# Score tiles as 64-row products on two row groups, and a batch's rows brought out of PSUM head by head on ScalarE

## The chip, the core and the metric

The kernel runs on one core of a Trainium2 chip. The metric is the device time of one launch, in microseconds, as a median of several runs. The core's engines are TensorE (in the profile PE for products and PEld for its weight loads), VectorE (DVE), ScalarE (ACT) and GpSimd (POOL); SP is the queue from which nearly all transfers are issued. Each engine works through its instructions in the order in which the program wrote them and waits at semaphores for the others.

## What is computed

The reference is attention with a top-32 mask, followed by a mixture of experts on its output:

```
scores = scale * q @ k.T                  # 8 batches, 8 heads, 576 tokens, 64 wide
kth    = 32nd largest of each row
attn   = softmax(where(scores >= kth, scores, -1e9))
x      = (attn @ v) as 4608 rows of 512
logits = x @ w_gate + modality_bias[modality_id]
e      = argmax(logits);  g = softmax(logits)[e]
out    = g * (relu(x @ w1[e]) @ w2[e])    # 8 experts, 1024 hidden
```

Everything is float32. The choice of the 32 largest and of the expert hangs on small differences, so the scores are computed to nearly full float32 precision.

## The kernel before

Two heads make a pair, and there are 32 pairs. The 1152 query rows of a pair are cut into nine tiles of 128 rows; tiles 0 to 7 belong to one head each (even tiles to head 0, odd ones to head 1), and tile 8 holds the last 64 rows of both heads. One step of the main loop (`for i in range(LAST)`, 288 tiles and some more) writes the work of several tiles at different stages: the scores of tile `i + 2`, the search for the 32nd largest of tile `i`, the probabilities, the transposes and the evacuation of earlier tiles, the product with v of an earlier pair, the preparation of the next pair, and a share of the expert work. Four pairs make a batch of 36 steps. The order on each engine is this program order; there is no scheduler behind it.

**Scores.** `prep` transposes q and k and splits each into a part `hi` of type float32r and the rest `lo` (`split`), into a tile `st` whose partitions 0 to 63 hold head 0 and 64 to 127 head 1. Six transfers on SP (`stack`, L313) then write `ks`, in which both halves of the 128 partitions hold the same 64 rows of k, and four more (L315) write `qs`, with `hi` of q in the lower half and `lo` in the upper. A product of 128 rows of `qs` with `ks` so adds two of the four terms hi·hi, lo·hi, hi·lo, lo·lo at once. `qk` (L371) makes a normal tile of four such products, two for each half of 288 key columns; tile 8 takes its q from `qbd`, in which the two heads stand apart (GpSimd, `fill`, L324), in four products of 512 columns and four of 64. The tile goes to one PSUM tile `S` of two banks (a single buffer), and ScalarE copies it to SBUF (`sevac`, L378). The first pair is scored without stacking, by 64-row products straight from its `st` (`unstacked`, L355), two tiles at a time: tile S from the lower row group, tile T from the upper.

**Other TensorE work of a step.** The transposes of the probabilities (L481), the transposes and the remainder of the split in `prep` (L290, L297, L276), the product with v in 64-column groups (`av`, L509), the gate's products in 32-column groups (L554), the turning back of a batch's rows (`xrow`, L542), and the experts (L775, L787).

**Rows of a batch.** When a batch's four pairs are done, five steps of `xrow` transpose its output back to token rows, and VectorE takes the PSUM tile X out, times 1 over the softmax sum `rd` (L543), as an entry of the list `late`.

**Pacing.** Expert work of slots of 256 rows stands in a list `moe`, and each step takes pieces from it as long as a balance is positive: the step adds `STEP` = 3.39 and takes off what the table `COST` says of its own TensorE work. A slot may begin when enough batches are done. Where the list is empty, or no batch is done yet, `keep_warm` issues a few products that nobody reads. Thirteen slots are done in this way; the rest come in a last part with products split in three terms (L1005, L1021).

Of the kernel before, what the change touches and what calls it, by code (L numbers as in the profile page):

```python
# [53 lines left out]
COST = {"trans": 0.5, "qk": 0.5, "mix": 1.02, "rest": 0.22, "t": 0.11, "prep": 0.43, "logits": 1.2, "xrow": 0.54, "av": 0.49, "av8": 0.17}  # L54
# [18 lines left out]
def kernel(  # L73
# [40 lines left out]

    LD, PR, T = {}, {}, {}
# [57 lines left out]
    qbd = [[o.tile([128, 128], FR, name=f"qbd{i}{j}", bufs=1) for j in range(2)] for i, o in enumerate((const, wk))]  # L173
    for a in qbd:
        for t in a:
            V.memset(t.bitcast(FT), 0.0)
# [88 lines left out]
    late, late_pe = [], []  # L265
# [14 lines left out]
    def prep(p, part, first=False):  # L280
# [3 lines left out]
        if first:  # L284
            d.setdefault("st", st0)
        elif "st" not in d:
            d["st"] = wk.tile([128, 2, 2, S], FR, name="st", bufs=1)
# [16 lines left out]
        if part == "k":  # L304
            d["ks"] = wk.tile([128, 2, 2, S], FR, name="ks", bufs=2)
        else:
            d["qs"] = wk.tile([128, 2, S], FR, name="qs", bufs=2)

        def stack(h, queues=(SP, SP)):
            for v in range(2):  # L310
                if part == "k":
                    for a, b, o in ((0, S, 0),) if h == 0 else ((0, 512, 64), (512, S, -512)):
                        queues[v].dma_start(d["ks"][half(v), :, h, a + o:b + o].bitcast(FT), st[half(h), :, a:b].bitcast(FT))  # L313
                else:
                    queues[v].dma_start(d["qs"][half(v), h, :].bitcast(FT), st[half(h), v, :].bitcast(FT))  # L315

        for h in range(2):
            f = lambda h=h, **o: stack(h, **o)
# [14 lines left out]
    st0 = wk.tile([128, 2, 2, S], FR, name="ks", bufs=2)  # L333
    bd0 = wk.tile([128, 2, S], FR, name="qs", bufs=2)[:, 0, :256].rearrange("p (x s) -> p x s", x=2)

    def fill_first():
        for h in range(2):
            r = slice(h * 64, h * 64 + 64)
# [717 lines left out]
    for i in range(LAST):  # L1056
# [25 lines left out]
        if ok(u):  # L1082
            sign(u)
# [320 lines left out]
```

## Time and profile before

| | |
|---|---|
| median of 3 runs | 1266.87 us (1263.65 to 1268.3) |
| the profiled execution | 1262.36 us, span 1260.6 us |
| TensorE busy (products) | 1181.1 us, 94% |
| VectorE busy | 1140.2 us, 90% |
| ScalarE busy | 989.0 us, 78% |
| GpSimd busy | 677.8 us, 54% |
| 16 DMA engines, mean share | 51.2% for SP's queue, 199.28 MB in all |

Busy time is the time in which an engine's instructions run as the profile has them. A product's record lasts until its result is out, and the next one starts well before that, so the rate of TensorE is read from the starts of its records and not from their lengths. A float32 product of 256 or 512 columns stands in the trace as two records. The span has a start of about 33 us, the main loop to about 1110 us, and the last part.

### The profile page before, as it was taken

What the parts mean: (1) busy time and instruction counts of PE and PEld (TensorE: products, weight loads), DVE (VectorE), ACT (ScalarE), POOL (GpSimd) and SP (SyncE); (2) the same over time, 40 slices, a digit from 0 to 9 for tenths busy, and PEclk for the clock granted to TensorE, in tenths of its full rate; (3) what the DMA queues carried; (4) which work ended last, traced back from release to release, by engine and by line L of the source; (5) the groups of instructions that cost most, each with busy time, mean ns of one, the idle gap of its engine ahead of it and who ended that gap; (6) DMA issues with size and microseconds to landing.
All of it is one profiled execution on the core that took longest, in us unless ns stands there. A gap on an engine that the chain in (4) does not pass through costs nothing. (4 is left out here: it accounts for less than half of the span.)

```text
span 1260.6 us, 28788 instructions
## 1 busy us (share of the span) xinstructions
PE 1181.1 (94%) x8032; PEld 927.0 (74%) x8032; DVE 1140.2 (90%) x5917; ACT 989.0 (78%) x2014; POOL 677.8 (54%) x1253
## 2 busy tenths in 40 slices
PE   7889987899988999989999999999999999999985
PEld 5667766768766868677777778787778775699885
DVE  6999999999999999999999999999999996477751
ACT  4999988889888988888898888888888885256542
POOL 4888865564574557554755466556755573211110
PEclk7999999999999999999999999999999999999998
DMA  4563337754356745655666566656576425478550
GB/s 107 156 186 86 87 86 224 199 150 126 86 136 188 217 117 157 189 156 139 171 184 177 146 182 191 185 154 169 161 207 178 128 71 168 150 251 275 190 174 15
DMA packets 204339, 199.28 MB, mean 158 GB/s; under 512 B 104413, under 2 KB 151533, under 8 KB 204160
## 3 DMA queue, kind: packets, MB, share of 16 engines
q1 hardware_dynamic: 196880, 177.96, 51.2%
q0 software_dynamic: 6080, 19.00, 4.2%
q8 instruction: 69, 1.13, 0.4%
q14 instruction: 110, 0.90, 0.2%
q10 hardware_dynamic: 1200, 0.30, 0.1%
HBM read 118.63 MB, written 24.23 MB: 113 GB/s over the span
## 5 line engine op out<-in xcount | busy, mean ns | idle before, releaser
L385 DVE MAX8 cand<-Ssb 128x8 f32<-128x82 f32 (+1 forms) x2016 | 429.5, 230 | 5.4 <-ACT Ssb L378 5.4
L423 POOL TENSOR_TENSOR y<-Ssb,K 128x576 f32<-128x576 f32 x288 | 370.4, 1286 | 5.7 <-ACT K L417 5.4
L417 ACT ACTIVATE K<-Ssb,n 128x576 bf16<-128x576 f32 x288 | 227.2, 789 | 29.0 <-POOL y L423 28.2
L378 ACT ACTIVATE Ssb<-S 128x576 f32<-128x576 f32 x284 | 185.9, 655 | 80.9 <-PE S L371 45.5
L371 PE MATMUL S<-ks,qs 128*128 128x288 f32 x992 | 220.3, 344 | 29.2 <-ACT Ssb L378 16.8
L427 DVE MAX8 mg<-y 128x8 f32<-128x576 f32 x288 | 214.7, 745 | 10.2 <-POOL y L423 10.2
L371 PEld LDWEIGHTS S<-ks,qs 128*128 128x128 f32 x992 | 151.5, 190 | 73.0 <-ACT Ssb L378 27.3
L775 PE MATMUL E<-xgT,w1b 128*128 128x256 f32 x816 | 196.8, 384 | 8.8 <-ACT hT L779 7.6
L441 ACT ACTIVATE ex<-Ssb,sm 128x576 f32<-128x576 f32 x256 | 199.9, 781 | 0.0
L489 ACT ACTIVATE PT<-T 128x640 f32<-128x640 f32 (+1 forms) x288 | 191.0, 663 | 5.6 <-PE T L481 5.6
L787 PE MATMUL E<-w2b,hT 128*128 128x512 f32 x400 | 188.2, 597 | 1.5 <-ACT hT L779 0.9
L447 DVE SCALAR_TENSOR_TENSOR P<-Ssb,kth,ex 128x576 f32<-128x576 f32 x224 | 188.0, 840 | 0.7 <-DVE cand L385 0.3
L481 PE MATMUL T<-idf,P 128*128 128x128 f32 x1152 | 170.4, 275 | 8.9 <-ACT P L466 8.9
L775 PEld LDWEIGHTS E<-xgT,w1b 128*128 128x128 f32 x816 | 147.5, 190 | 32.8 <-ACT hT L779 11.3
L470 POOL TENSOR_SCALAR spare<-P 1x1 f32<-1x1 f32 x224 | 50.0, 223 | 202.3 <-DVE mg L396 189.2
L481 PEld LDWEIGHTS T<-idf,P 128*128 128x128 f32 x1152 | 135.0, 140 | 17.9 <-ACT P L466 13.5
L509 PE MATMUL X<-PT,vm 128*64 128x256 f32 (+1 forms) x1536 | 145.0, 331 | 1.5 <-ACT xT L512 0.9
L410 POOL TENSOR_SCALAR n<-mg 128x1 f32<-128x1 f32 x288 | 72.8, 253 | 111.5 <-DVE mg L398 103.2
L509 PEld LDWEIGHTS X<-PT,vm 128*64 128x64 f32 x1536 | 88.4, 137 | 47.2 <-issue 10.2
L787 PEld LDWEIGHTS E<-w2b,hT 128*128 128x128 f32 x400 | 69.8, 190 | 59.7 <-issue 53.9
L1027 POOL DMA_INDIRECT out_dram<-ot,tk x12 | 12.0, 1000 | 106.7 <-ACT ot L1026 106.7
L396 DVE MAX8 mg<-cand 128x8 f32<-128x56 f32 x288 | 60.9, 211 | 0.2
(233 smaller groups left out, 2245.1 us busy)
## 6 DMA issues: line engine op xcount, KB each, us to landing
w1b<-in_moe_w_dram SPq DMA_DIRECT2D x76, 512.0 KB, 5.4
w2b<-in_moe_w_dram SPq DMA_DIRECT2D x76, 512.0 KB, 5.3
ks<-st SPq DMA_DIRECT2D x62, 288.0 KB, 3.4
qs<-st SPq DMA_DIRECT2D x124, 144.0 KB, 2.7
ks<-st SPq DMA_DIRECT2D x62, 256.0 KB, 4.8
xg<-xs SPq DMA_DIRECT2D x19, 516.0 KB, 5.1
km<-in_k_dram SPq DMA_DIRECT2D x64, 128.0 KB, 3.4
vm<-in_v_dram SPq DMA_DIRECT2D x32, 256.0 KB, 3.4
```

What stands on the lines that cost most here:

```text
L371: PE.matmul(ps[:, hf, u - a:v - a], l, d["ks"][:, x, h, u + o:v + o], start=(n == 0), stop=(n == len(terms) - 1), skip_group_check=(j == 8))
L385: return [lambda s=s: V.max(c[:, s * 8:s * 8 + 8], T[i]["S"][:, bnd[s]:bnd[s + 1]]) for s in range(NSUB)]
L417: A.activation(t["K"], t["S"], AF.Sign, scale=2.0 ** -24 - 1.0, bias=t["n"][:, 1, i % 3:i % 3 + 1], accum_out=t["n"][:, 0, i % 3:i % 3 + 1])
L423: G.tensor_tensor(t["y"], t["S"], t["K"], op=OP.mult)
L427: V.max(t["mg"][:, i % 3, 24:32], t["y"])
L441: A.activation(t["ex"], t["S"], AF.Exp, bias=t["s"][:, i % 3:i % 3 + 1])
L447: V.scalar_tensor_tensor(t["P"], t["S"], kth[:, i:i + 1], t["ex"], op0=OP.is_ge, op1=OP.mult, accum_out=dn)
L481: PE.transpose(T[i]["pt"][:, x, :], (Pm if c == 4 else Pb[c % 2])[:, h * 512 + x * 128:h * 512 + x * 128 + 128], idf)
L489: A.activation(o, T[i]["pt"][:, :n], AF.Copy)
L509: PE.matmul(o.rearrange("p (a b) -> p a b", a=2) if j < 8 else o, l, r, start=(c == 0), stop=(c == 4))
L775: PE.matmul(ps[:, f % 2], w1b[:, c, f * 128:(f + 1) * 128], xgT[:, c, :], start=(c == 0), stop=(c == KC - 1))
L787: PE.matmul(o["py"], hT[:, f, t * 128:(t + 1) * 128], w2b[:, f, :], start=(f == 0), stop=(f == FC - 1))
```

## The change

A normal score tile is made of six products of 64 rows in place of four of 128. The two halves of the key columns are worked on by the two halves of TensorE's rows: row group 0 (partitions 0 to 63) makes columns 0 to 287 and row group 1 columns 288 to 575, in two banks, in turn, and the term lo·lo is left out, so that each half takes three products. For a tile of head 0 the lower half reads `st` itself; the upper half needs head 0's q and the second half of its k in partitions 64 to 127, and reads a new tile `sw`, which holds what has to cross to the other half (and the reverse for head 1). `cross` fills it with five transfers for a pair. Tile 8 reads `st` in six 128-row products of 288 columns. `st` has two buffers now, `ks` and `qs` are gone. The first pair is scored as before but with three terms. In batches 1 to 6, `xrow` gives its PSUM tile to ScalarE: eight copies of 64 columns, one for each head, with that head's column of `rd` as the scale, four in the next step and four in the step after it (lists `xev` and `slower`). The table `COST` has 0.4 for `qk` (0.5 before) and 0.8 for `mix`, tile 8 (1.02 before).

```diff
-COST = {"trans": 0.5, "qk": 0.5, "mix": 1.02, ...
+COST = {"trans": 0.5, "qk": 0.4, "mix": 0.8, ...
+    TERMS = ((0, 0), (0, 1), (1, 0))
...
-            d["st"] = wk.tile([128, 2, 2, S], FR, name="st", bufs=1)
+            d["st"] = wk.tile([128, 2, 2, S], FR, name="st", bufs=2)
...
-        def stack(h, queues=(SP, SP)):
-            for v in range(2):
-                if part == "k":
-                    for a, b, o in ((0, S, 0),) if h == 0 else ((0, 512, 64), (512, S, -512)):
-                        queues[v].dma_start(d["ks"][half(v), :, h, a + o:b + o].bitcast(FT), st[half(h), :, a:b].bitcast(FT))
-                else:
-                    queues[v].dma_start(d["qs"][half(v), h, :].bitcast(FT), st[half(h), v, :].bitcast(FT))
+            d["sw"] = wk.tile([128, 2, 512 + 288], FR, name="sw", bufs=2)
+        def cross(h):
+            if part == "q":
+                cols = ((0, 512, 0),)
+            else:
+                cols = ((288, S, 512),) if h == 0 else ((512, S, 512), (0, 224, 576))
+            for a, b, o in cols:
+                SP.dma_start(d["sw"][half(1 - h), :, o:o + b - a].bitcast(FT), st[half(h), :, a:b].bitcast(FT))
...
     def fill(p, bd):
         for h in range(2):
-            G.tensor_scalar(bd[h][:, h * 64:h * 64 + 64], PR[p]["qs"][:, h, 512:].bitcast(FT), 1.0, 1.0,
-                            op0=OP.mult, op1=OP.mult)
+            r = slice(h * 64, h * 64 + 64)
+            G.tensor_scalar(bd[r, :, r], PR[p]["st"][r, :, 1, 512:].bitcast(FT), 1.0, 1.0, op0=OP.mult, op1=OP.mult)
...
     def qk(i, p, j, bd):
-        for hf in range(2):
-            a, b = (hf * 288, hf * 288 + 288) if j < 8 else ((0, 512), (512, S))[hf]
-            if j < 8:
-                c, h = divmod(j, 2)
-                terms = [(d["qs"][:, h, c * 128:(c + 1) * 128], x, h, a, b, 0) for x in range(2)]
-            else:
-                terms = [(bd[0], x, 0, a, b, 0) for x in range(2)]
-                for u, v, o in ((a, min(b, 512), 64), (512, b, -512)):
-                    terms += [(bd[1], x, 1, u, v, o) for x in range(2)] if u < v else []
-            for n, (l, x, h, u, v, o) in enumerate(terms):
-                PE.matmul(ps[:, hf, u - a:v - a], l, d["ks"][:, x, h, u + o:v + o], start=(n == 0),
-                          stop=(n == len(terms) - 1), skip_group_check=(j == 8))
+        c, h = divmod(j, 2)
+        for x, y in TERMS:
+            for g in range(2):
+                r = slice(g * 64, g * 64 + 64)
+                if j == 8:
+                    l, m = bd[:, x, :], st[:, y, 0, g * 288:g * 288 + 288]
+                elif g == h:
+                    l, m = st[r, x, 1, c * 128:c * 128 + 128], st[r, y, 0, h * 224:h * 224 + 288]
+                else:
+                    l, m = d["sw"][r, x, c * 128:c * 128 + 128], d["sw"][r, y, 512:]
+                PE.matmul(ps[:, g, :288], l, m, start=(x + y == 0), stop=(x == 1), skip_group_check=True)
...
     def xrow(u, c, xTb, x5b):
+        if FAST <= u < B - 1:
+            def heads(a):
+                for h in range(a, a + HP):
+                    A.activation(x5b[:n_, c, h * D:(h + 1) * D], ps[:n_, h // 2, (h % 2) * D:(h % 2 + 1) * D], AF.Copy,
+                                 scale=RD[u][:n_, h // 2, 2 * c + h % 2:2 * c + h % 2 + 1])
+            xev.append(lambda: heads(0))
+            slower.append(lambda: heads(HP))
+            return
...
+        ripe, slower[:] = slower[:], []
         while xev:
             xev.popleft()()
+        xev.extend(ripe)
```

On TensorE, in the step of the main loop that holds the gate's products of a middle batch, the order before was this (E is an expert's PSUM tile, S the scores, T the transposed probabilities, X the shared one):

```order
L775 MATMUL E<-xgT,w1b 128x256 x4
L371 MATMUL S<-ks,qs 128x288 x4
L481 MATMUL T<-idf,P_124 128x128 x5
L554 MATMUL X<-xT,wgt 32x512 x4
L554 MATMUL X<-xT,wgt 32x64 x4
```

In the changed kernel the same place reads:

```order
L770 MATMUL E<-xgT,w1b 128x256 x4
L360 MATMUL S<-st 128x288
L360 MATMUL S<-sw 128x288
L360 MATMUL S<-st 128x288
L360 MATMUL S<-sw 128x288
L360 MATMUL S<-st 128x288
L360 MATMUL S<-sw 128x288
L468 MATMUL T<-idf,P_120 128x128 x5
L549 MATMUL X<-xT,wgt 32x512 x4
```

The four products of 128 rows have become six of 64 rows, the two row groups in turn, between expert products and transposes of 128 rows that are the same as before. Over a batch of 36 steps in the middle of the loop, TensorE's order passes from one kind of group to another (whole array, row groups, 64-column groups, 32-column groups) 18 times before and 78 times now. The expert work counts thirteen slots in both.

On ScalarE, in a step of a middle batch in which a row tile is taken out, the order before was (K the comparison with the 24th value, ot an expert's output, ex the exponential, PT the transposed probabilities):

```order
L417 ACTIVATE K,n<-Ssb,n 128x576
L797 ACTIVATE ot<-E,sgt_141 128x512
L746 ACTIVATE xgT<-X 128x512
L441 ACTIVATE ex<-Ssb,sm 128x576
L378 ACTIVATE Ssb<-S 128x576
L489 ACTIVATE PT<-T 128x640
```

and now is:

```order
L404 ACTIVATE K,n<-Ssb,n 128x576
L533 ACTIVATE x_152<-X,rd 128x64 x4
L792 ACTIVATE ot<-E,sgt_137 128x512
L741 ACTIVATE xgT<-X 128x512
L428 ACTIVATE ex<-Ssb,sm 128x576
L365 ACTIVATE Ssb<-S 128x576
L476 ACTIVATE PT<-T 128x640
```

Four copies of 64 columns stand ahead of the exponential, of the copy of the scores and of that of the transposes; there are two such steps for each of the thirty row tiles, and the thirty products on VectorE (L543) are gone there.

On SP, the transfers that prepare a pair were, in the middle of the loop (w2b is an expert's weights):

```order
L313 DMA ks<-st 64x2x576 x2
L313 DMA ks<-st 64x2x512
L313 DMA ks<-st 64x2x64
L313 DMA ks<-st 64x2x512
L313 DMA ks<-st 64x2x64
L717 ISA
L717 DMA w2b<-in_moe_w_dram 128x2x512
L315 DMA qs<-st 64x576 x4
```

and are now:

```order
L312 DMA sw<-st 64x2x288
L312 DMA sw<-st 64x2x64
L312 DMA sw<-st 64x2x224
L712 ISA
L712 DMA w2b<-in_moe_w_dram 128x2x512
L312 DMA sw<-st 64x2x512 x2
```

Ten issues for a pair have become five, at the same place among the others.

## Rows read from the trace of the kernel before

**Rows 1.** Stages: start:end, length, busy PE PEld DVE ACT POOL, PEclk, DMA share, GB/s
```profile
33.00:173.00 140.00, 125.11 (x1025) 99.85 (x1024) 140.00 (x772) 131.86 (x300) 114.59 (x157) 0.99 0.52 131
245.00:373.00 128.00, 125.20 (x853) 94.82 (x852) 123.73 (x666) 111.69 (x232) 77.46 (x144) 1.00 0.53 140
373.00:507.00 134.00, 124.97 (x878) 98.69 (x876) 132.94 (x726) 114.63 (x235) 74.42 (x144) 1.00 0.59 164
507.00:642.00 135.00, 130.06 (x861) 100.30 (x860) 132.04 (x736) 115.19 (x235) 77.96 (x150) 0.99 0.61 166
642.00:906.00 264.00, 261.31 (x1743) 201.67 (x1742) 258.42 (x1407) 229.60 (x472) 159.07 (x305) 1.00 0.62 171
906.00:1040.00 134.00, 131.16 (x872) 100.45 (x870) 131.36 (x719) 114.69 (x235) 80.62 (x155) 1.00 0.52 148
```
**Rows 2.** Timeline of a normal tile: start us, length us, engine, line, what, count
```profile
705.32 0.88 PE L371 MATMUL S<-ks,qs 128*128 128x288 f32 x4
705.51 0.32 PEld L371 LDWEIGHTS S<-ks,qs 128*128 128x128 f32 x2
706.03 0.71 PE L481 MATMUL T<-idf,P 128*128 128x128 f32 x5
```
**Rows 3.** Timeline of TensorE around a tile 8
```profile
700.95 1.64 PE L371 MATMUL S<-ks,qbd 128*128 128x512 f32 x8
702.42 0.65 PE L481 MATMUL T<-idf,P 128*128 128x128 f32 x4
```
**Rows 4.** Timeline: 64-row products of the first pair, S and T on different row groups
```profile
7.71 0.33 PE L355 MATMUL S<-ks 64*128 64x288 f32 x1
7.77 0.35 PE L355 MATMUL T<-ks 64*128 64x224 f32 x1
7.88 0.33 PE L355 MATMUL S<-ks 64*128 64x288 f32 x1
7.96 0.41 PE L355 MATMUL T<-ks 64*128 64x288 f32 x1
```
**Rows 5.** Timeline: into 64-column groups (first two rows), and out of them
```profile
616.13 0.27 PE L290 MATMUL X<-idf,kqt 128*128 128x128 f32 x1
616.33 0.44 PE L509 MATMUL X<-PT,vm 128*64 128x256 f32 x2
...
619.22 0.79 PE L371 MATMUL S<-ks,qs 128*128 128x288 f32 x4
619.85 0.27 PE L481 MATMUL T<-idf,P 128*128 128x128 f32 x1
```
**Rows 6.** Timeline: out of the first pair's row groups (first two rows), and into them
```profile
25.08 0.30 PE L355 MATMUL T<-ks 64*128 64x288 f32 x1
25.31 0.19 PEld L276 LDWEIGHTS X<-st,nid 128*128 128x128 f32 x1
...
21.52 1.05 PE L297 MATMUL X<-idf,qm 128*128 128x128 f32 x4
22.51 0.28 PEld L355 LDWEIGHTS S<-ks 64*128 64x128 f32 x1 [0.33 <-issue]
```
**Rows 7.** VectorE's line that takes a batch's rows out: count, ns min/median/max
```profile
L543 DVE TENSOR_TENSOR x<-X,rd x40: 660/671/692, 169.2 to 1080.3; 128x512 f32<-128x512 f32 x32, 64x512 f32<-64x512 f32 x8
```
**Rows 8.** ScalarE's groups by shape: count, busy us, mean ns, idle before
```profile
L779 ACT ACTIVATE hT<-E 128x512 f32<-128x512 f32 x51 | 30.6, 600 | 16.2 <-PE E L775 15.6
L797 ACT ACTIVATE ot<-E,sgt 128x512 f32<-128x512 f32 x25 | 17.2, 686 | 8.1 <-PE E L787 8.0
L512 ACT ACTIVATE xT<-X 128x64 f32<-128x64 f32 x32 | 7.2, 224 | 5.0 <-PE X L509 5.0
```
**Rows 9.** Waits: us in total, times, longest; and TensorE's timeline at one of them
```profile
PE S L371 <- DMA qs<-st: 12.2, 6, 3.9
...
539.25 0.77 PE L371 MATMUL S<-ks,qs 128*128 128x288 f32 x4 [2.90 <-DMA qs<-st]
```
**Rows 10.** Stage of the first pair's 64-row products; the third figure from the right is PEclk
```profile
11.00:19.00 8.00, 7.58 (x42) 6.27 (x42) 6.75 (x49) 2.45 (x6) 4.20 (x11) 0.50 0.34 88
```

More of the change, by code (lines that the diff above doesn't have):

```diff
@@ L53 @@
 AV7 = (0, 5)
-COST = {"trans": 0.5, "qk": 0.5, "mix": 1.02, "rest": 0.22, "t": 0.11, "prep": 0.43, "logits": 1.2, "xrow": 0.54, "av": 0.49, "av8": 0.17}
+COST = {"trans": 0.5, "qk": 0.4, "mix": 0.8, "rest": 0.22, "t": 0.11, "prep": 0.43, "logits": 1.2, "xrow": 0.54, "av": 0.49, "av8": 0.17}
 RN = 6
@@ L171 @@
     G.iota(tokc[:, 4:5], pattern=[[1, 1]], base=512, channel_multiplier=1, allow_small_or_imprecise_dtypes=True)
[L173 to L176, printed above, removed]
+    qbd = [o.tile([128, 2, 128], FR, name=f"qbd{i}", bufs=1) for i, o in enumerate((const, wk))]
+    for t in qbd:
+        V.memset(t.bitcast(FT), 0.0)
     Pb = [wk.tile([128, 2 * S], FT, name=f"P{i}", bufs=1) for i in range(2)]
@@ L262, in routing_loads @@
         pad_rows(E)
-    late, late_pe = [], []
+    late, late_pe, slower = [], [], []
     nxt = deque()
@@ L283, in prep @@
         d = PR.setdefault(p, {})
-        if first:
-            d.setdefault("st", st0)
-        elif "st" not in d:
-            d["st"] = wk.tile([128, 2, 2, S], FR, name="st", bufs=1)
+        if "st" not in d:
+            d["st"] = wk.tile([128, 2, 2, S], FR, name="st", bufs=2)
         if part == "t":
@@ L331, in flush @@
             x.clear()
[L333 to L338, printed above, removed]
-            G.tensor_scalar(bd0[r, :, r], PR[0]["st"][r, :, 1, 512:].bitcast(FT), 1.0, 1.0, op0=OP.mult, op1=OP.mult)
     def unstacked(j):
@@ L344, in unstacked @@
             return
[L345 removed]
+        ps = [psS.tile([128, 2, 512], FT, name="S"), psT.tile([128, 2, 512], FT, name="T")]
+        st = PR[0]["st"]
         for h, t in enumerate(ps):
             T[j + h] = {"ps": t[:, :, :288]}
[L348 to L356 removed]
+        for x, y in TERMS:
+            for h, a, b, o in ((0, 0, 288, 0), (1, 0, 64, 512), (1, 64, 288, -64), (0, 288, S, 0), (1, 288, S, -64)):
+                r = slice(h * 64, h * 64 + 64)
+                PE.matmul(ps[h][:, a // 288, a % 288:a % 288 + b - a], st[r, x, 1, j * 64:j * 64 + 128],
+                          st[r, y, 0, a + o:b + o], start=(x + y == 0 and a % 288 == 0), stop=(x == 1),
+                          skip_group_check=True)
@@ L373, in qk @@
-        T[i] = {"ps": ps[:, :, :288] if j < 8 else ps.rearrange("p a b -> p (a b)")[:, :S]}
+        c, h = divmod(j, 2)
+        for x, y in TERMS:
+            for g in range(2):
[7 more added lines that the diff above has]
+                PE.matmul(ps[:, g, :288], l, m, start=(x + y == 0), stop=(x == 1), skip_group_check=True)
@@ L936 @@
         prep(0, part, True)
-    fill_first()
+    fill(0, qbd[0])
     modality = bias_loads()
@@ L1069, in scores @@
                 pp, jj = divmod(i + QL, 9)
-                if pp == 0:
+                if pp == 0 and jj < 8:
                     unstacked(jj)
```

22 lines of the change are left out of this document (4 added, 18 removed).

## The prediction

> **What bounds the kernel now.** The chain of waits of the page follows only the last output transfers, so I read the loop by stages first [rows 1]: one stretch is about one batch of 36 tiles, 642 to 906 holds two. From 33 to 173 us VectorE is busy all of 140.0 us and TensorE idles 14.9. From 245 us on the expert work has filled TensorE too: it idles 2.8, 9.0, 4.9, 2.7 (for two batches) and 2.8 us, while VectorE idles 4.3, 1.1, 3.0, 5.6 and 2.6. From 507 us on what counts is therefore TensorE, with VectorE close behind and ScalarE at 87%.
>
> A busy share of TensorE includes tails, so next I read the timeline for what a score tile takes of the stream [rows 2]: the first of its four products is dispatched at 705.32, takes over when its weights' successor starts to load at 705.51, and the transposes begin at 706.03. That is 0.52 us, 0.13 a product, with every weight load hidden behind the product ahead of it. A tile 8 runs from 700.95 to 702.42 [rows 3]; less the same 0.19 of the product before it, 1.28.
>
> **TensorE, what is saved.** Two row groups do work at once: S products of 288 columns start 0.17 apart while T products of 224 and 288 columns run between them [rows 4]; with the two streams in step I take 0.13 for a pair. A normal tile is three pairs, 0.39 for 0.52. Tile 8 is six whole-array products, 0.78 for 1.28. A batch has 32 and 4 of them: 32 x 0.13 + 4 x 0.50 = 6.2 us less.
>
> **TensorE, what is added.** Where products go from one kind of group to another, the trace shows a gap. Without a change a 128-column transpose follows the last after (0.71 - 0.27) / 4 = 0.11 [rows 2, 5]; into 64-column groups it takes 0.20 [rows 5], so 0.09 is lost. Out of the first pair's row groups the same is seen: the last product, dispatched at 25.08, streams 0.13, and the next load starts at 25.31, 0.10 later [rows 6]. That load is then not hidden: out of the column groups, the tile's first dispatch is 0.63 before the transposes (619.22 to 619.85) and not 0.52, so 0.11 more [rows 5]. Together 0.2 us a change. Into row groups at full clock there is no row. At the half clock the last of four transposes spaced (1.05 - 0.42) / 3 = 0.21 ends at 22.37, and the row group's load starts 0.14 later [rows 6]; so I price the entry like the exit, 0.205. The bounds are nothing for the entry and, above, row groups that do not overlap at all.
>
> [...]
>
> The order shows 18 such changes a batch before and 78 after, 60 x 0.205 = 12.3 us more. TensorE's batch grows by 12.3 - 6.2 = 6.1 us. The lower `COST` moves expert pieces by a step or so; their number stays, so I cost that at nothing: the idle time above is what would cover it.
>
> **Where that lands.** From 33 to 173 us (five pairs) TensorE gets 80 changes, 16.4 - 5.2 - 2.5 = 8.7 us, inside its 14.9 of idle time beside a full VectorE: nothing. Stretch by stretch after that, growth less idle: 245 to 373, 3.3; 373 to 507, nothing (9.0 idle); 507 to 642, 4.1, because 2.9 of its 4.9 is one wait for a transfer [rows 9] and covers nothing; 642 to 906, 12.2 - 2.7 = 9.5; 906 to 1040, 3.3. Sum **+20.2 us**.
>
> **VectorE.** Thirty products of 0.671 us go [rows 7], 20.1 us, 3.4 a batch. Where TensorE is full that is worth nothing; only from 373 to 507 does VectorE (132.9 of 134) still decide, and there TensorE comes up to 131: **-2 us**.
>
> **ScalarE.** A 64-column copy takes 0.224 us, and a scale read per partition adds 0.686 - 0.600 = 0.086 [rows 8]: 0.31 a head, 2.5 us a row tile, 12.4 a batch on top of 114.8. It comes in ten steps of 36, 1.24 us in each, ahead of the copies of scores and transposes for which TensorE and VectorE wait. Were none of it hidden it would be 74 us, were all of it, nothing. ScalarE idles 0.48 us a step on average and TensorE's steps get longer, so most is hidden; I take 1 us a batch, **+6 us**.
>
> [...]
>
> **Transfers and start.** Ten issues on SP become five for a pair, in the same place; nothing new is queued behind them. Of the 12.2 us that TensorE waits for `qs`, six times [rows 9], I count 5 as gone: the 2.9 at 536 us, where TensorE is full, and half of the longest; the rest stands where VectorE decides. **-5 us**. In the first pair a quarter of the products goes. The granted clock there was 0.50 of full, the lower level [rows 10], so a product takes twice 0.13; two of them in each row group for four groups of tiles are 2.1 us: **-2 us**. The copies on GpSimd for `qbd` keep their number and are hidden.
>
> Sum: 20.2 - 2 + 6 - 5 - 2 = +17.2 us on the profiled execution's 1262.4, 1279.6. That execution lies 4.5 us under the median of the runs; the median I forecast is **1284 us**, slower. About 0.5% (6.3 us) is what a measurement of this kernel can tell from no change.
>
> **Rivals.**
> - *Changing groups is nearly free.* If a change costs under 6.2 / 60 = 0.10 us, for instance because the row groups are entered without a gap, TensorE's batch gets no longer. At 0.10, what is left is the start and the waits, -7: 1260. At nothing, VectorE's 20.1 counts, held to about half by a ScalarE that then has 127 of 130 us a batch: -10 - 7, 1250. For it: no row shows the entry at full clock. Against it: three rows show a gap, one of them out of row groups. [...] Chance 0.13 near nothing, 0.08 near 0.10.
> - *ScalarE becomes the bound.* If half of the 1.24 us is waited for in each of sixty steps, 37 us come in place of 6: 1315. For it: three engines near full. Against: there was 13% of ScalarE to spare. Chance 0.05.
> - *The clock falls.* While TensorE worked on 64-row products for 7.58 of 8 us the granted clock stayed at 0.50 [rows 10]. From 33 to 173 us TensorE has least else to do; a third of its 134 us at that level is 45 more, less 6 of idle time: 1323. Against: only an eighth of a step is spent on row groups now. Chance 0.04.
> - *The halves do not run together* in the loop, so the change does not do what it says: 0.39 more for 32 tiles, 12.5 us a batch, over five and a half batches 69 us: 1353. [Rows 4] speak against it. Chance 0.04.
>
> **How the numbers follow.** The forecast has 0.66, with a range of its own from 1270 to 1302 (a change at 0.17 to 0.24 us, ScalarE 0 to 12). From 1256 to 1312 the range leaves out the case of free changes and most of the last three, 2 in 10. Faster by over 0.5% are free changes and some of those near 0.10: 0.16. Within 0.5%: the rest of them and the forecast's lower end, 0.14. Slower: 0.70.
>
> **What would show it.** In the changed profile: 0.13 us between pairs of score products; 0.1 us between an expert product's end and the tile's first load, and as much before the transposes, so about 0.8 us a tile for 0.52; a batch from 642 us on of 136 to 138 us for 132; TensorE's idle time near nothing there, VectorE's up to some 8 us a batch. It is wrong if the tile takes under 0.6 us, if TensorE waits for ScalarE's copies of scores, or if PEclk falls in the loop.

## The result

The change took 1281.71 us (median of four runs, 1280.42 to 1282.38) against 1265.26 for the kernel before on the same chip: 16.5 us more, ratio 1.0127 with an interval from 1.0107 to 1.0146. The forecast was 1284, with a range from 1256 to 1312. The sum came out, and by luck: the experiments show that its parts did not, and that a part priced at nothing, the order of the expert work, makes a third to a half of it.

The page of the changed kernel gives, for the engines and the first queue:

```profile
PE 1206.4 (94%) x8438; PEld 870.2 (68%) x8438; DVE 1140.8 (89%) x5884; ACT 1035.1 (81%) x2254; POOL 678.8 (53%) x1253
...
q1 hardware_dynamic: 182496, 148.49, 40.9%
```

TensorE is busy 25 us longer in 18 us more of span, ScalarE 46 us longer. VectorE lost thirty products of 0.67 us and is as busy as before, because other records of the same work got longer: those of the masked probabilities (`P`) from 840 to 883 ns in the mean, 9.7 us in all; what makes them longer is not shown. SP's queue has 40.9% instead of 51.2%.

The same stages as in [rows 1], after:

```profile
33.00:173.00 140.00, 122.73 (x1068) 90.03 (x1067) 140.00 (x762) 129.67 (x292) 114.17 (x154) 0.99 0.35 93
245.00:373.00 128.00, 124.38 (x887) 83.62 (x886) 121.54 (x662) 117.02 (x267) 75.82 (x146) 1.00 0.35 95
373.00:507.00 134.00, 126.19 (x929) 90.33 (x927) 132.68 (x733) 122.28 (x277) 75.15 (x145) 1.00 0.48 136
507.00:642.00 135.00, 133.11 (x915) 91.47 (x913) 131.89 (x732) 120.57 (x273) 78.64 (x151) 1.00 0.50 140
642.00:906.00 264.00, 258.01 (x1781) 176.39 (x1782) 249.26 (x1324) 234.96 (x535) 154.30 (x294) 1.00 0.48 136
906.00:1040.00 134.00, 130.82 (x897) 89.86 (x894) 126.58 (x681) 117.90 (x267) 76.18 (x146) 1.00 0.47 135
```

From 642 to 906 us VectorE idles 14.7 us where it idled 5.6, as forecast. But TensorE idles 6.0 where it idled 2.7, and "near nothing" was forecast. If its longer stream were the whole cause, that idle time would have gone. This is the first sign that the batch got longer for more than one reason. The granted clock (third figure from the right) is 0.99 to 1.00 in all of these stretches, the upper of the two levels in this trace (the lower is 0.50, as in [rows 10]), so the rival in which the clock falls is out.

TensorE's timeline of the change, a tile 8, the expert products after it and a normal tile:

```profile
701.95 1.15 PE L360 MATMUL S<-st,qbd 128*128 128x288 f32 x6
702.94 0.60 PE L468 MATMUL T<-idf,P 128*128 128x128 f32 x4
704.07 2.86 PE L770 MATMUL E<-xgT,w1b 128*128 128x256 f32 x12 [0.54 <-ACT hT L774]
706.86 0.40 PE L360 MATMUL S<-st 64*128 64x288 f32 x1
706.87 0.41 PE L360 MATMUL S<-sw 64*128 64x288 f32 x1
707.10 0.29 PE L360 MATMUL S<-st 64*128 64x288 f32 x1
707.11 0.30 PE L360 MATMUL S<-sw 64*128 64x288 f32 x1
707.23 0.29 PE L360 MATMUL S<-st 64*128 64x288 f32 x1
707.25 0.29 PE L360 MATMUL S<-sw 64*128 64x288 f32 x1
707.47 0.76 PE L468 MATMUL T<-idf,P 128*128 128x128 f32 x5
```

The two halves of a pair start 0.01 to 0.02 us apart (0.003 to 0.004 in the median of 228 tiles), so they do run together, and the rival in which they do not is out. The second pair follows the first by 0.24, the third by 0.13, the transposes by 0.24: the two changes of group stand in the 0.11 too much after the first pair, the 0.11 too much ahead of the transposes, and a gap ahead of the first pair. The last belongs to the expert products' end: counted over the 83 tiles of this kind, the time from the last 256-column expert product to the first transpose is 0.903 us in the median, against 0.744 over 82 tiles before, and the second transpose follows the first by 0.165 instead of 0.108. A normal tile's own share is therefore 0.903 - 0.215 + 0.057 = 0.745 for 0.744 - 0.215 = 0.529. Tile 8 takes 1.019 between the same neighbours for 1.507. A batch has 32 x 0.216 - 4 x 0.488 = 5.0 us more stream.

What TensorE waits for most at the scores, before (us in total, times, longest), beside the wait of [rows 9]:

```profile
PE S L371 <- ACT Ssb L378: 20.9, 25, 2.4
```

and after, with the expert work:

```profile
PE S L360 <- ACT Ssb L365: 17.3, 24, 2.1
...
PE E L770 <- ACT hT L774: 5.6, 11, 1.1
...
PE S L360 <- DMA sw<-st: 0.8, 1, 0.8
```

The wait for `qs` [rows 9], 12.2 us, has become 0.8 for `sw`. The others name ScalarE. The wait for its copies of scores was to be a sign that the forecast is wrong; it got shorter, 17.3 us for 20.9, and after 507 us only 0.8 of it is left.

For what follows I use two marks. A "batch" is the time between the starts of ScalarE's copies of scores of tile 0 of pair 20 and of pair 24; the "loop" ends at the last such copy, whose row in ScalarE's timeline is, before:

```profile
1034.68 0.66 ACT L378 ACTIVATE Ssb<-S 128x576 f32<-128x576 f32 x1
```

and after:

```profile
1050.76 0.65 ACT L365 ACTIVATE Ssb<-S 128x576 f32<-128x576 f32 x1
```

The batch as a stretch, with the columns of [rows 1], before:

```profile
642.10:774.00 131.90, 130.72 (x873) 100.91 (x872) 129.27 (x704) 114.81 (x237) 79.58 (x153) 1.00 0.62 171
```

and after, 6.2 us longer:

```profile
640.70:778.80 138.10, 135.11 (x928) 93.04 (x929) 130.69 (x699) 122.44 (x277) 80.02 (x153) 1.00 0.48 136
```

The loop got 16.1 us longer, the rest (to the end of the span) 228.0 for 225.9. Both are of single profiled executions, which lie up to 4 us off the medians of their kernels, so such differences are good to a few us. Up to pair 8 the change is 5.1 us ahead (240.0 for 245.1); from there on it loses.

### The profile page after: what moved, and what is told of

Its sections match the earlier page's. It is cut to its first block, busy times and chain, and to the rows that moved or that the text cites. A ratio compares the mean times of both kernels' runs of the same rounds, so it can differ in the third digit from the quotient of the medians.

```text
span 1278.8 us, 29517 instructions
## 1 busy us (share of the span) xinstructions
PE 1206.4 (94%) x8438; PEld 870.2 (68%) x8438; DVE 1140.8 (89%) x5884; ACT 1035.1 (81%) x2254; POOL 678.8 (53%) x1253
## 3 DMA queue, kind: packets, MB, share of 16 engines
q1 hardware_dynamic: 182496, 148.49, 40.9%
## 5 line engine op out<-in xcount | busy, mean ns | idle before, releaser
L428 ACT ACTIVATE ex<-Ssb,sm 128x576 f32<-128x576 f32 x256 | 204.0, 797 | 0.0
L476 ACT ACTIVATE PT<-T 128x640 f32<-128x640 f32 (+1 forms) x288 | 195.0, 677 | 8.7 <-PE T L468 7.6
L434 DVE SCALAR_TENSOR_TENSOR P<-Ssb,kth,ex 128x576 f32<-128x576 f32 x224 | 197.8, 883 | 3.7 <-ACT ex L428 3.0
L468 PE MATMUL T<-idf,P 128*128 128x128 f32 x1152 | 180.5, 284 | 11.8 <-ACT P L453 11.3
L360 PE MATMUL S<-st 64*128 64x288 f32 x744 | 165.4, 328 | 10.8 <-ACT Ssb L365 10.4
L360 PE MATMUL S<-sw 64*128 64x288 f32 x744 | 164.5, 328 | 6.4 <-ACT Ssb L365 4.1
L468 PEld LDWEIGHTS T<-idf,P 128*128 128x128 f32 x1152 | 123.9, 141 | 53.5 <-issue 25.0
L360 PEld LDWEIGHTS S<-st 64*128 64x128 f32 x744 | 106.9, 186 | 63.3 <-ACT Ssb L365 18.1
L457 POOL TENSOR_SCALAR spare<-P 1x1 f32<-1x1 f32 x224 | 43.0, 192 | 195.5 <-DVE mg L383 176.7
L360 PEld LDWEIGHTS S<-sw 64*128 64x128 f32 x744 | 106.8, 186 | 44.3 <-issue 15.8
```

Source lines behind the costliest of these rows:

```text
L360: PE.matmul(ps[:, g, :288], l, m, start=(x + y == 0), stop=(x == 1), skip_group_check=True)
L428: A.activation(t["ex"], t["S"], AF.Exp, bias=t["s"][:, i % 3:i % 3 + 1])
L434: V.scalar_tensor_tensor(t["P"], t["S"], kth[:, i:i + 1], t["ex"], op0=OP.is_ge, op1=OP.mult, accum_out=dn)
L468: PE.transpose(T[i]["pt"][:, x, :], (Pm if c == 4 else Pb[c % 2])[:, h * 512 + x * 128:h * 512 + x * 128 + 128], idf)
L476: A.activation(o, T[i]["pt"][:, :n], AF.Copy)
```

## The experiments

All differences of time are between the kernel's median and that of the kernel before on the same chip. Ratios are to the kernel before.

**1. Scores alone.** The change with every row tile of `x` on VectorE again:

```diff
-        if FAST <= u < B - 1:
-            def heads(a):
...
-            slower.append(lambda: heads(HP))
-            return
```

> The changed kernel with the rows of all batches taken out on VectorE again; only the scores part of the change is left. Theory (TensorE pays 0.2 us for each change between row groups and whole array, and that is nearly all of the loss): a batch from 640 us on takes 135 to 138 us, against 138.1 in the changed kernel and 131.9 before, and the median is 1272 to 1282, so 10 us or more above before. Rival (ScalarE's copies of 64 columns are the loss): 1262 to 1267, as before.

Measured: 1274.95 us, ratio 1.0071 (1.0048 to 1.0095), +9.6 us, and a batch of 136.1 us, both as the theory said. The run keeps the lower costs.

**2. Heads alone.** The kernel before with the heads on ScalarE:

```diff
+        if FAST <= u < B - 1:
+            def heads(a):
...
+            slower.append(lambda: heads(HP))
+            return
```

> The kernel before with the eight copies of 64 columns on ScalarE for batches 1 to 6, and nothing else of the change. Theory: TensorE's work is that of before, so the median is 1260 to 1270, within 5 us of before; VectorE's 3.4 us a batch show where VectorE decides, ScalarE's 2.9 us in two steps of seven show as short waits. Rival (ScalarE is the loss): 1275 to 1285.

Measured: 1262.61 us, ratio 0.9975 (0.9959 to 0.999), -2.8 us, in the theory's range. So the scores with the lower costs cost 9.6 and the heads gain 2.8 alone, but the two together cost 16.5: 9.7 us are in neither. The trace of the second run has a clue in the expert work behind the loop. One of the six groups of its 256-column products, before:

```profile
L1005 PE MATMUL X<-xgh,w1h 128*128 128x256 f32 x144 | 41.2, 286 | 3.2 <-ACTq L1298 3.2
```

and in run 2:

```profile
L1013 PE MATMUL X<-xgh,w1h 128*128 128x256 f32 x168 | 48.4, 288 | 3.5 <-ACTq L1308 3.5
```

All six together have 672 records for 576 (the 665 and 570 of a later expectation are miscounted). The planner gives expert work a credit for each entry of `late`; with the heads these entries are gone, and one expert block of 256 rows had left the loop.

**3. Six whole-array products in a normal tile.** No change of group, but both heads' rows added up in the scores:

```diff
...
-                elif g == h:
-                    l, m = st[r, x, 1, c * 128:c * 128 + 128], st[r, y, 0, h * 224:h * 224 + 288]
                 else:
-                    l, m = d["sw"][r, x, c * 128:c * 128 + 128], d["sw"][r, y, 512:]
+                    l, m = st[:, x, 1, c * 128:c * 128 + 128], st[:, y, 0, g * 288:g * 288 + 288]
```

> The changed kernel with each normal tile made of six products of the whole array, 128 rows of st for both heads at once, in the same order and banks; so the scores are those of two heads added and not the reference's, and sw is filled but not read. No change between kinds of groups, but no two products at once: 6 x 0.13 = 0.78 us a tile in place of the measured 0.39 and two changes of 0.2. Theory: the two are about equal, 1275 to 1285. Rival (row groups run together and a change costs little): this kernel loses 0.39 us on 32 tiles of each batch, 12.5 us, and comes to 1330 or more.

Measured: 1291.54 us, ratio 1.0211 (1.0179 to 1.0243), +26.2 us, 9.7 more than the change: above the theory's range of 1275 to 1285, and far below the rival's. The timeline shows the tile:

```profile
705.47 1.06 PE L358 MATMUL S<-st 128*128 128x288 f32 x6
706.37 0.71 PE L466 MATMUL T<-idf,P 128*128 128x128 f32 x5
```

Between the same neighbours as above it takes 1.011 - 0.215 = 0.796 us, 0.05 more than the change's 0.745; times 248 tiles that is 12.6. So three pairs with two changes of group cost nearly what six products one after the other cost, and the pairs do overlap: without that the change would have been where this run is, or worse.

**4. Three whole-array products.** Half of the products of a normal tile left out, no change of group:

```diff
...
+                    l, m = st[:, x, 1, c * 128:c * 128 + 128], st[:, y, 0, g * 288:g * 288 + 288]
+                if j < 8 and (x == 1 or (y == 1 and g == 1)):
+                    continue
...
```

> As the kernel with six whole-array products, but with three a tile (two for the first half of the columns, one for the second), so half of the products of a normal tile are left out: 0.39 us of TensorE and no change between kinds of groups. It stands for what the row groups would give if changing to them were free. Theory: TensorE's batch falls by 12 us to about 123 us, VectorE (some 126 us a batch) or ScalarE (122) becomes the bound, a batch from 640 us on takes 127 to 131 us, and the median is 1235 to 1255. Rival (VectorE, ScalarE or the transfers hold the changed kernel where it is): 1270 or more.

Measured: 1252.29 us, ratio 0.99 (0.987 to 0.9931), -13.1 us. A tile takes 0.40 us, 0.35 less than in the change, 11 us a batch; the batch is only 5.7 us shorter (132.4). The batch as a stretch shows TensorE with 5.9 us of idle time:

```profile
629.70:762.10 132.40, 126.54 (x833) 95.09 (x832) 128.57 (x703) 120.97 (x277) 78.59 (x153) 1.00 0.51 143
```

That is outside the 127 to 131 us of the theory, though the median is inside its range: cheaper scores alone do not bring the batch below about 132 us here. A tile at 0.39 us is what the rival of free changes assumed, and its price for it, 1250, is close to the 1252 of this run; that rival failed by the cost of the changes and not by its sum.

**5. The planner's costs of before.** The change with one line of its diff undone:

```diff
-COST = {"trans": 0.5, "qk": 0.4, "mix": 0.8, ...
+COST = {"trans": 0.5, "qk": 0.5, "mix": 1.02, ...
```

> The change with the planner's costs of before (qk 0.5, mix 1.02 instead of 0.4, 0.8), everything else as in the change. The written order then holds one block of 256 expert rows fewer in the loop; the loop over the rest takes it up at the end, as it did in the run with the heads alone (665 of its 256-column products recorded instead of 570). Theory M: TensorE is full in the loop, so the moved block takes 24 us off the loop (62 products of 0.215 us and 25 of 0.43) and adds 12 us behind it (237.7 us from the loop's end to the last instruction in the heads-alone run against 225.9): 1267 to 1273 us. Rival: the costs only shift expert work between steps and the total stays, 1279 to 1285 us.

Measured: 1269.31 us, ratio 1.0032 (1.0021 to 1.0042), +3.4 us, as theory M said. Two numbers in a table, and the block that they move, are worth 13 of the change's 16.5 us. The loop ends at 1028.1, 22.7 earlier than in the change; the rest takes 237.0, 9.0 more. The block is not the whole of the 22.7. Up to the loop's end the change has these expert products, of 256 columns and of 512 (the first figure in brackets is the count of their records):

```profile
0.00:1050.76 1050.76, 182.40 (x754) 136.08 (x755) 0.99 0.45 125
0.00:1050.76 1050.76, 164.80 (x352) 61.75 (x352) 0.99 0.45 125
```

and run 5:

```profile
0.00:1028.11 1028.11, 170.21 (x704) 126.92 (x704) 0.99 0.45 125
0.00:1028.11 1028.11, 158.50 (x337) 58.70 (x338) 0.99 0.45 125
```

A record of 256 columns holds 0.215 us of the stream, one of 512 holds 0.43. A block, 64 and 32 records, is 27.5 us and not 24; of these 50 and 15 records, 17.2 us, stood ahead of the loop's end. So some 5 of the 22.7 us have another source. What else the two numbers change is the order of the pieces that stay.

**6. Heads, block kept.** The kernel of run 2 with the change's costs:

```diff
-COST = {"trans": 0.5, "qk": 0.5, "mix": 1.02, ...
+COST = {"trans": 0.5, "qk": 0.4, "mix": 0.8, ...
```

> The heads-alone kernel (scores of before) with the costs of the change, so that the loop holds as many expert blocks as before. Theory M: the heads on ScalarE cost 1 to 2 us a batch in the steady batches, and the 2.8 us that the heads-alone run was faster came from the block that its planner moved behind the loop; with the block back in the loop 1270 to 1280 us. Rival: the heads relieve VectorE and the gain is theirs, 1259 to 1266 us.

Measured: 1275.53 us, ratio 1.0071 (1.0049 to 1.0092), +9.6 us, as theory M said. The gain of run 2 came with the moved block. But this run changes two things against the kernel before, the heads and the order of the expert work (by the lower costs and by the credit that the heads no longer give); run 9 parts them.

**7. The kernel before, block moved.**

```diff
-COST = {"trans": 0.5, "qk": 0.5, ...
+COST = {"trans": 0.5, "qk": 0.56, ...
```

> The kernel before with one number changed, the planner's cost of a score tile, 0.56 instead of 0.5, which moves one expert block behind the loop and nothing else. Theory M: 24 us off the loop and 12 us on behind it, 1250 to 1258 us. Rival: the loop is held by VectorE (98% busy in it), the block in it is nearly free, and moving it out only adds to the end: 1268 to 1277 us.

Measured: 1267.2 us, ratio 1.001 (0.9993 to 1.0027). It lies between the two theories, nearer to the rival. The loop ends 7.0 us earlier (1027.7) and the rest takes 10.0 more (235.9). As in run 5, some 17 us of the block's stream (50 and 16 records) leave the loop. Here 7.0 of them come back, in run 5 all of them and some 5 us more. So most of the block is covered in the kernel before, where VectorE is nearly as full, and on the path in the change; that TensorE has the bound alone there is my reading, since the costs also move the pieces that stay. Against this run, with the same expert products in each batch, run 2 is 4.1 us better in the medians (-2.8 against +1.3); the two profiled executions do not show it (1266.67 and 1265.24), so that the heads pay there is likely and not shown.

**8. One change of group more in each direction.** A whole-array product with zero weights between the first and the second pair of each normal tile:

```diff
...
                 PE.matmul(ps[:, g, :288], l, m, start=(x + y == 0), stop=(x == 1), skip_group_check=True)
+            if j < 8 and x + y == 0:
+                PE.matmul(ps[:, 0, :288], zer, st[:, 0, 0, :288], start=False, stop=False, skip_group_check=True)
```

> The change with one more product in each of the 248 normal tiles of pairs 1 to 31: a whole-array product of 288 columns whose weights are zero, between the first and the second pair of 64-row products, so that each tile leaves and enters the row groups once more. By the gaps in the trace of the change (0.087 and 0.056 us on leaving, 0.094 and 0.104 on entering, 0.34 together) and 0.13 for the product itself: 0.47 us a tile, 117 us if all of it is on the path, less what VectorE hides in the first batch: 1375 to 1400 us. By the prediction's 0.205 a change: 0.54 a tile, up to 1416. Rival (a change costs nothing, the tiles are slow for another reason): the product alone, 0.13 a tile, 1305 to 1316 us.

Measured: 1361.93 us, ratio 1.0763 (1.0742 to 1.0785), 79.5 us above the change. TensorE's timeline, with the first product of each pair:

```profile
761.09 0.40 PE L362 MATMUL S<-sw 64*128 64x288 f32 x1
...
761.42 0.40 PE L364 MATMUL S<-st,zer 128*128 128x288 f32 x1
761.75 0.40 PE L362 MATMUL S<-sw 64*128 64x288 f32 x1
...
761.98 0.29 PE L362 MATMUL S<-sw 64*128 64x288 f32 x1
...
762.21 0.77 PE L472 MATMUL T<-idf,Pm 128*128 128x128 f32 x5
```

Out to the product 0.33, back 0.33, the next pair 0.23 and not 0.13. From the last expert product to the first transpose it is 1.428 for 0.903: 0.525, of which 0.13 is the product and 0.395 the two changes, 0.20 each. My 0.34 for both in the expectation was too low, since I had left out that the pair behind the new entry also comes 0.10 late, as the second pair does in every tile of the change; the prediction's 0.205 fits. The total lies under both ranges, and above the rival's: 0.32 us for each of the 248 tiles, because not every tile is on the path. In the batch it is 13.3 us (151.4 for 138.1) where 32 x 0.525 is 16.8, and of the 3.5 between them most is idle time that TensorE has used up: 3.0 us in the batch of the change (138.10 less 135.11), 0.4 here:

```profile
683.70:835.10 151.40, 151.00 (x960) 100.74 (x961) 135.11 (x700) 124.42 (x277) 80.42 (x153) 1.00 0.46 126
```

**9. Heads at the old order.** Run 2 with a credit for each of its row tiles as the entries of `late` had given it, so that TensorE's order is that of before:

```diff
             slower.append(lambda: heads(HP))
+            late_credit.append(1)
...
-        spare_pe += STEPS["small"] * len(small_) + (STEPS["late"] + STEPS["more"] * (len(lo) - 1) if lo else 0.0)
+        spare_pe += STEPS["small"] * len(small_) + (STEPS["late"] + STEPS["more"] * (len(lo) + cr - 1) if lo or cr else 0.0)
```

> The kernel before with the heads on ScalarE and nothing else: the planner is credited for each of those row tiles as for VectorE's multiplication before, so that TensorE's written order is that of before, instruction for instruction, with the same expert blocks in the loop. Theory P: what made the heads-with-block run 10 us slower than before were the change's lower costs, which overfill the steps; at the order of before the heads are worth nothing or a little, 1259 to 1267 us. Rival: the heads themselves cost on ScalarE once the loop holds all its expert blocks, 1271 to 1278 us.

Measured: 1267.92 us, ratio 1.0014 (1.0001 to 1.0027), +1.8 us: a little above theory P's range, far under the rival's. The heads by themselves cost 1.8 us. Run 6 has the same heads and the order of the change, by the lower costs and without the credit, and stands 7.8 higher. The batch of run 9, with the columns of [rows 1]:

```profile
641.40:774.90 133.50, 131.20 (x873) 100.99 (x872) 129.85 (x699) 121.10 (x276) 78.74 (x152) 1.00 0.62 170
```

The same stretch of run 6:

```profile
642.90:778.40 135.50, 132.07 (x873) 100.94 (x872) 129.63 (x699) 121.23 (x276) 77.94 (x152) 1.00 0.60 167
```

The same 873 products, and every engine's busy time is the same within 0.9 us; run 6 takes 2.0 longer. What differs is which step holds which expert product. TensorE's timeline of the same three steps, run 9:

```profile
655.32 1.88 PE L796 MATMUL E<-w2b,hT 128*128 128x512 f32 x4
656.63 1.10 PE L371 MATMUL S<-ks,qs 128*128 128x288 f32 x4
...
658.55 1.02 PE L796 MATMUL E<-w2b,hT 128*128 128x512 f32 x2
...
659.77 0.77 PE L371 MATMUL S<-ks,qs 128*128 128x288 f32 x4
```

and run 6:

```profile
656.81 2.74 PE L795 MATMUL E<-w2b,hT 128*128 128x512 f32 x6
658.98 1.09 PE L371 MATMUL S<-ks,qs 128*128 128x288 f32 x4
...
661.53 0.80 PE L371 MATMUL S<-ks,qs 128*128 128x288 f32 x4
```

A product of 512 columns stands in two records, so one of them holds 0.43 us. In run 6 the planner's balance has room for six records in the first step and leaves none for the second. Between the copies of scores the first step grows from 2.93 to 4.50 us, the second shrinks from 4.10 to 3.49 only: a step that gets less on TensorE still has the work of the other engines. In the two batches from pair 20 on, 14 of the 72 gaps between one score tile and the next hold no expert product in run 6, 10 in run 9 and in the kernel before. The waits in the batch, run 6 (run 9 has the first of them, with the same 1.5, none on `issue`, and 0.5 on VectorE's `ex` in all):

```profile
PE X L509 <- ACT xgT L754: 1.5, 1, 1.5
...
PE S L371 <- issue: 0.5, 1, 0.5
...
DVE Pm L447 <- ACT ex L441: 2.3, 2, 1.6
```

**10. The change, costs as measured.**

```diff
-COST = {"trans": 0.5, "qk": 0.4, "mix": 0.8, ...
+COST = {"trans": 0.5, "qk": 0.73, "mix": 0.84, ...
```

> The change with the planner's costs set to what a score tile takes in the trace of the change, 0.73 for a normal tile and 0.84 for the ninth; two expert blocks fewer than the change in the loop. One block behind the loop was worth 12.4 us (22.7 off the loop, 9 to 10 on behind it). Theory M (TensorE still bounds the loop): the second block is worth as much again, 1256 to 1260 us. Rival: without it VectorE takes over, as in the kernel before, where a moved block took 7 us off the loop and added 10 behind it: 1266 to 1274 us.

Measured: 1274.34 us, ratio 1.0069 (1.0052 to 1.0086), just above the rival's range. Two blocks more than in the change are behind the loop. Against run 5 the second took 15.8 us off the loop (1012.3) and added 23.1 behind it (260.1). Neither theory had the price behind the loop right: the first block is cheap there (9 to 10 us), the second is not. With the exact cost of a tile the kernel is 4.8 us slower than with the costs of before.

**11. Heads, two blocks moved.**

```diff
-COST = {"trans": 0.5, "qk": 0.5, ...
+COST = {"trans": 0.5, "qk": 0.72, ...
```

> The heads-alone kernel (scores of before) with a planner's cost of 0.72 for a score tile, so that two expert blocks fewer stand in the loop than in the kernel before (the heads-alone run had one fewer). Theory M: VectorE and ScalarE hold the loop, so the second block takes 4 to 8 us off it and adds 10 behind it: 1263 to 1270 us. Rival: TensorE still holds it, and the block takes 15 to 24 us off: 1249 to 1257 us.

Measured: 1275.8 us, ratio 1.0078 (1.0057 to 1.0098): out of both ranges. Against run 2 the loop ends 11.6 earlier (1015.7), the rest takes 21.5 more (259.2). It confirms the second block's price.

**12. Scores at the old order.** Run 1 with the costs of before; all products but the scores' stand where they stood:

```diff
-COST = {"trans": 0.5, "qk": 0.4, "mix": 0.8, ...
+COST = {"trans": 0.5, "qk": 0.5, "mix": 1.02, ...
```

> The change's score products alone: rows of x on VectorE as before, and the planner's costs of before, so that on TensorE every product other than the scores' stands where it stood before. Theory S: the group changes cost TensorE 5.8 us of stream a batch, of which the kernel pays what it paid from the heads-with-block run to the change (6.2 us in all), and the lower costs pay the rest of the 9.6 us that scores with the lower costs were slower: 1269 to 1273 us. Rival: the lower costs harm only beside the heads, and the scores bring the whole 9.6 us or more by themselves: 1274 to 1282 us.

Measured: 1269.65 us, ratio 1.0039 (1.0024 to 1.0054), +4.5 us, as theory S said. The batch of run 12:

```profile
638.40:773.20 134.80, 134.13 (x928) 92.90 (x929) 129.59 (x705) 115.67 (x236) 79.46 (x152) 1.00 0.48 139
```

and that of run 1:

```profile
644.60:780.70 136.10, 134.77 (x929) 92.90 (x929) 131.58 (x704) 115.76 (x236) 78.27 (x152) 1.00 0.48 138
```

At the old order TensorE idles 0.7 us of a batch: here its stream sets the time. The lower costs add 1.3 us a batch with the same number of products.

The runs make two ways from the kernel before to the change:

| step | scores first | heads first |
|---|---|---|
| scores in row groups | +4.5 (run 12) | +6.9 (run 6 to the change) |
| order of the expert work | +5.1 (run 12 to run 1: lower costs) | +7.8 (run 9 to run 6: lower costs, no credit) |
| heads on ScalarE | +6.9 (run 1 to the change: heads, no credit) | +1.8 (run 9) |
| sum | 16.5 | 16.5 |
| batch, from 131.9 | 134.8, 136.1, 138.1 | 133.5, 135.5, 138.1 |

Each time is known to 1.6 to 3 us either way. Which steps are clean is seen in TensorE's order. With the score products of a tile counted as one, TensorE's products stand in the same order, one by one, in the kernel before and runs 9 and 12; in a second order, again the same in all, in the change and runs 3, 4, 6 and 8; in a third in runs 2 and 5. Run 1 has an order of its own, neither that of before nor that of the change. So the way with heads first is the clean one: heads 1.8 at the old order, the order 7.8, scores 6.9 at the new order. In the other way the last 6.9 holds the heads and a second change of order together. The scores are measured at three orders, +4.5, +6.1 (run 2 to run 5, from -2.76 to +3.37) and +6.9, which the intervals do not tell apart. That a part costs more once TensorE's slack is used up by another would fit all this and is not shown by it. The kernel before with the lower costs alone was not run.

## Why the prediction was right, and where it was not

*What bounds the kernel.* "From 507 us on what counts is TensorE, with VectorE close behind": right in the order, too sure. Of some 17 us of expert stream taken out of the loop, 7.0 came back (run 7). The kernel before has a double bound, TensorE busy for 261.3 and VectorE for 258.4 of 264 us [rows 1], and its slack does not show in these busy times.

*Saved on TensorE.* Pairs at 0.13 and tile 8 at 0.78: right. Tile 8 takes 0.80 and gives 0.488 of the forecast 0.50, and the third pair starts 0.13 after the second.

*The change of group.* Forecast 0.205 each, entry like exit, without a row for the entry at full clock. Measured 0.355 for two in the change (0.745 less three pairs), 0.18 each, and 0.20 each in run 8. The first of the rivals, nearly free changes, is out by this. The stream of a batch grew by 5.0 us, forecast 6.1; at 0.18 instead of 0.205 sixty changes are 1.5 less. Within a pair the second product starts 3 to 4 ns behind the first in the median; three such pairs at 0.13 alone would make a tile of 0.39 us, and it takes 0.745.

*Where it lands.* This is the first step that failed. I took growth less idle time, 20.2 us, with the idle time of busy records: 1.35 us a batch from 642 us on. With the scores alone at the old order the five stretches from pair 8 on grew by 1.2, 0.8, 0.1, 5.6 and 1.7, together 9.4, where I had 20.2 (the growth of 5.0 a batch cost 2.9 in the batch, 134.8 for 131.9). The third of them also lost the wait of 2.9 us for `qs`, which the forecast booked under transfers, so 17.3 is the figure to compare. About 2 us a batch were covered and not 1.35, and growth was smaller by 1.1; and in the stretches before 642 us more was covered than I counted. Taking growth less idle time was right, but the idle time was read from records, which are longer than their share of the stream: a 128-column transpose has 0.27 us, and the next starts after 0.11 [rows 2, 5].

*"The lower `COST` moves expert pieces by a step or so; their number stays, so I cost that at nothing."* This is the step that was wrong. Their number stayed, as said, and the order alone cost 5.1 us (runs 12, 1) and 7.8 (runs 9, 6). The prediction also left out that the heads take away the credit of `late`, the other half of the new order. The planner was told 0.4 for a tile that had become 0.745, and run 6 shows that the order costs beside the old tiles of 0.529 too: some steps get more than fits and others nothing.

*VectorE.* Thirty products gone, no gain where TensorE sets the time: right. The 2 us forecast from 373 to 507 us came to 0.8 in run 9 (pairs 12 to 16, 133.4 for 134.2). The change's VectorE idles 7.4 us a batch; forecast up to 8.

*ScalarE.* Forecast 0.31 us a head, 12.4 a batch, of which 1 us a batch is paid, +6. On the path the heads with VectorE's relief cost 1.8 us (run 9), where -2 + 6 = 4 was forecast; the price of a head was wrong. ScalarE's groups in the change:

```profile
L533 ACT ACTIVATE x<-X,rd 128x64 f32<-128x64 f32 x192 | 46.6, 368 | 0.0
```

By its mean a head has 0.37 us, but heads start 0.197 apart (median of 180 neighbours), and in the timeline four of them hold the engine for 0.78:

```profile
706.30 0.99 ACT L533 ACTIVATE x<-X,rd 128x64 f32<-128x64 f32 x4
707.08 0.87 ACT L428 ACTIVATE ex<-Ssb,sm 128x576 f32<-128x576 f32 x1
```

That is 40 x 0.195 = 7.8 us a batch, and ScalarE's busy time in the batch rose by 7.6 (122.44 for 114.81; by 6.3, to 121.10, with the heads alone in run 9). My 0.31 was made of the lengths of records, and the next record starts before one ends: 0.37 us long, they start 0.195 apart. The rival in which ScalarE becomes the bound is out: ScalarE idles 15.7 us a batch.

*Transfers and start.* The wait of 12.2 us is gone but for 0.8, and the start of pair 1 is 5.2 us earlier (28.1 for 33.3). Of that, 1.0 is left at pair 3 (85.7 for 86.7), since VectorE is full from 33 to 173 us, busy 140.0 of 140 in both kernels. From there to pair 8 the kernel before waits 3.9 us for `qs` and the change 0.8 for `sw`; at pair 8 the change is 5.1 ahead, scores alone at the old order 5.8. Forecast were 7, of which 2.9 at 536 us; the size was nearly right, the place earlier.

*The sum.* 20.2 - 2 + 6 - 5 - 2 = 17.2 stands against 16.5, by the clean steps 1.8 for the heads, 7.8 for the order, 6.9 for the scores with transfers and start. In the forecast's terms TensorE, transfers and start were 13.2 and measured 6.9 (4.5 at the old order); the heads with VectorE were 4 and measured 1.8; the order was 0 and measured 7.8. Errors of opposite sign made a good total: the number was right by luck, the mechanism in part. Of the signs named ahead, the tile (0.745 us for about 0.8), the batch (138.1 us for 136 to 138) and VectorE's idle time came, TensorE's idle time near nothing did not.

*Not settled.* Heads and lost credit together cost 6.9 us from run 1 to the change. In the profiled executions 2.2 of that lies in the loop and 3.1 behind it (228.0 for 224.9 in run 1), where no head is left. The 3.1 is expert work on the other side of the mark: run 1 has 768 and 353 expert records ahead of the loop's end and the change 754 and 352, 3.4 us of stream less. So the loop lost more than the 2.2 shows; how much of that is the heads and how much the order is open. Why the first block behind the loop costs 9 to 10 us and the second 21 to 23 is measured and not explained.

*A better version.* Of the kernels that compute all of it, run 2, the old scores with heads and one block moved, is the best: 0.9975 of the kernel before, with its profiled execution above its median (1266.67 for 1262.61). That is under the 0.5% that I called a difference. Tile 8's six products beside the old stacked `ks` and `qs` would by these rows save 0.49 us four times a batch, an estimate; this was not tried.

## What to carry to other kernels

Where a list of costs decides in which step work stands, a changed operation has to be priced twice, once on its engine and once through the order that its cost makes: run the change with the old table before judging the change. Packing products into row groups has to be weighed against the way in and out: here a visit saves three products of 0.13 over running its six in turn and spends 0.36 on going in and out, and against four stacked products it loses. Where two engines are as close as TensorE and VectorE here, price a term by taking a known amount of work out of the loop: what comes back tells how much of the stream is on the path. Count what really left, and keep the rest in its order: a block moved by a cost moves other pieces as well.

## What the runs showed that I had not expected

Some 17 us of expert stream taken out of the loop, with the costs that do it, are worth 7.0 us in the kernel before and 22.7 in the change, more than was taken out. A second block behind the loop costs 21 to 23 us where the first costs 9 to 10. Copies of 64 columns on ScalarE start 0.195 us apart while each record has 0.37. And the order of the expert pieces, with the same number of products on TensorE, is worth 5 to 8 us; lowering two of the planner's numbers by 0.1 and 0.22 us makes the 5 by itself.
